# Adaptive LayerNorm, linear attention and a gated MLP on one core: a new planner model, LayerNorm transposes on TensorE, Ln/Exp reciprocals

## The chip, the cores and the metric

The kernel runs on one core of one Trainium2 chip. A core has TensorE (PE, matrix products into PSUM), VectorE (DVE), ScalarE (ACT), GpSimd (POOL) and SyncE (SP, which here only issues DMAs). The metric is the device time of one launch in microseconds. Each engine works through its own queue in the order in which the program put instructions there, and waits on semaphores for the other engines.

## The reference

One batch of S = 2048 rows, D = 512, H = 32 heads of 16, F = 1376. A condition vector c gives six vectors of scale, shift and gate.

```python
mod = silu(c) @ w_mod                  # sa, ca, ga, sb, cb, gb
h = layernorm(x) * (1 + ca) + sa
x = x + ga * A(h)
h = layernorm(x) * (1 + cb) + sb
x = x + gb * B(h)

# A: q, k, v = h @ wqkv, then per head
phi(p) = concat(softmax(p @ w_phi), softmax(-p @ w_phi))
kv = sum_s phi(k)^T v;  z = sum_s phi(k)
o = (phi(q) kv) / (phi(q) . z + 1e-6);  A = o @ wo
# B
B = (sigmoid(h @ w_gate) * (h @ w_up)) @ w_down
```

All of phi(k) of the 2048 rows goes into kv and z before the first row of the output can be formed. Nothing behind it can start sooner except the queries.

## The kernel before

Rows are worked on in 16 tiles of 128. The program is not written in order: `Graph.add` collects some thousand tasks, each with the engines that may run it and a duration for each, what it reads and writes, its buffers, a due time `due` and an earliest time `rel`. `Graph.order` (L87) plays the tasks through on a model of the engines: at each model time, the free engine takes the ready task that is due first, and due times are pulled forward from the tasks that depend on it (L93). The order that comes out is the order of each engine's queue on the chip. In this model a task that ends frees its successors after `LAT` = 0.25 us, a transfer takes 1.9 us and its bytes at 380 GB/s, and VectorE and GpSimd don't disturb each other.

**Start.** Weights and x come over SP's queue (L544 to L557), x in four loads of four tiles. c is turned into its SiLU (c1 to c3), with a Tanh on ScalarE. The rows of w_mod give the shift and scale columns `modc` (L591, `modc1` for the first LayerNorm). w_phi is folded into the weights of k and q: transposes `tp_w` (L609) or DMA transposes (L619), products `fold_ps` (L626), copies into `wqk_f` (L632, L634).

**Tile loop.** For groups of four tiles: statistics (`st1`, L647 and L648, VectorE), 1/sqrt as a power on GpSimd (`rs1`, L653 and L654), normalised `xn` (L665 ScalarE, L667 VectorE, L669 GpSimd), a transpose into `h1T` (groups 0 and 1 on TensorE, `tp_h` L681; groups 2 and 3 by DMA, L672) and the modulation (`hm1`, L687 VectorE, L689 GpSimd, L691 ScalarE). Where xn isn't made by VectorE, `nmr` (L657) prepares minus mean times 1/sqrt. Then for each tile: K (L706), exponentials e and its inverse (L719, ScalarE), their sums over a head (L722) and reciprocals (L730) on VectorE, the product `phi` on GpSimd (L725, the last two tiles in halves that VectorE may take), V (L710), its copy `vaug` (L734), and the sum into `kvacc` (L278). The queries (Q, L767, in four blocks of four tiles; exponentials `eT`, L772), `ga` and `gb` (L744), and the products `wo` (L751) and `wd` (L756) with the gates lie beside it.

**From kv to the feed-forward stage.** `kvbd` is the masked copy of the sums (L290, L295). For each unit (tile 0, tile 1, then pairs): `sm` (L338) gives norm and denominator parts, `smS` is their copy (L342), `m`, `den`, its reciprocal and `cc` (L348 to L351) the factors. `num` (L363), `u` (L369), for tiles 0 and 1 a transposing product `tpo` and its copy (L380, L383), for the others their sum `o` on GpSimd (L387) and a DMA transpose (L390); the output `a_ps` (L396), the residual x1 (L401), its statistics (L405), `rs2` (L412, L413), `xn` (L428, L430), its transpose (`tp_x` L443 or by DMA, L435) and modulation (L450, L452).

**Feed-forward.** Chunks of 1, 1, 2, 4, 4 and 4 tiles: for each of 11 column blocks of F `g_ps` and `u_ps` (L471), tanh (L475, sigmoid as a half tanh), the gated product `hm` (L480, into the space of w_mod, two chunk buffers), then `y` (L491), which needs `wd`, the last residual (L500) and the store (L502). A bound on the exponents (L513 to L532) selects a safer second version of the whole, which is not run with these inputs.

Of the kernel before, what the change touches and what calls it, by code (L numbers as in the profile page):

```python
# [9 lines left out]
FP32 = mybir.dt.float32  # L10
BF16 = mybir.dt.bfloat16
# [19 lines left out]
QREL = [42.0, 50.0, 56.0, 64.0]  # L31
AREL = [0.0, 0.0, 62.0, 70.0, 77.0, 90.0, 100.0, 115.0, 125.0]
# [15 lines left out]
class Task:  # L48
    def __init__(self, name, alts, fn, due, rel, bufs, nbytes):
        self.name, self.alts, self.fn, self.due, self.rel = name, alts, fn, due, rel  # L50
        self.bufs, self.nbytes = bufs, nbytes
        self.deps, self.succ = set(), []
        self.ready = rel
        self.ndep = 0


class Graph:


    LAT = 0.25  # L60
    PE_OUT = 0.2
# [6 lines left out]
    def add(self, name, alts, fn, r=(), w=(), bufs=(), due=1e6, rel=0.0, nbytes=0):  # L68
        t = Task(name, alts, fn, due, rel, list(bufs), nbytes)
# [17 lines left out]
    def order(self):  # L87
# [8 lines left out]
        free_at = {e: 0.0 for e in ("PE", "ACT", "DVE", "POOL", "SP")}  # L96
        slots = {c: list(range(n)) for c, n in self.caps.items()}
        ready = [t for t in self.tasks if t.ndep == 0]
        events = [0.0]
        done = []  # L100
        out = []
        fifo = 0.0
        now = 0.0
        left = len(self.tasks)
        while left:
# [14 lines left out]
            held = set()  # L120
            for t in list(ready):
# [18 lines left out]
                free_at[e] = now + t.alts[e]  # L140
                t.end = free_at[e]
                if t.nbytes:
                    fifo = max(now + 1.9, fifo) + t.nbytes / 380e3
                    t.end = fifo
# [24 lines left out]
def kernel(  # L169
# [39 lines left out]
    flag = cst.tile([1, 1], INT32, name="flag")  # L209
    wmod_sb = cst.tile([P, KT, 6 * D], BF16, name="wmod_sb")  # L210
# [33 lines left out]
    pool.memset(mhalf[:], -0.5)  # L244

# [56 lines left out]
    def downstream(G, eT, base, first):  # L302
# [9 lines left out]
        for k in range(NC):  # L312
            for ft in range(FT):
# [4 lines left out]
                tm += {0: 0.3, 1: 0.3, 2: 0.5, 3: 0.4, 4: 0.4, 5: 0.0}[k]  # L318
        ydue = tm

        for p, tiles in enumerate(UNITS):
# [3 lines left out]
            d0 = gdue[k, 0] - 2.0  # L325
            rel = AREL[p] if first else 0.0
            sm = bank("sm", [P, 2, 256])
            smS = small("smS", [P, 2, 128])
# [13 lines left out]
            G.add(f"smS{p}", {"ACT": 0.16 + 0.11 * nt}, lambda e, sm=sm, smS=smS, nt=nt: act.copy(smS[:, 0:nt], sm[:, 0:nt, 0:128]), r=[("sm", p)], w=[("smS", p)], bufs=[sm, smS], due=d0)  # L342
# [536 lines left out]
```

## Time and profile before

| | |
|---|---|
| Time, median of 3 runs | 233.52 us (233.03 to 233.52) |
| The profiled execution's own time | 232.49 us |
| Its span, first to last instruction | 230.8 us |
| Mean granted clock of TensorE in the span | 0.982 |
| Busy: PE, DVE, ACT, POOL | 206.3, 172.3, 103.1, 82.4 us |
| Moved by DMA | 19.27 MB |

The profile shows one execution. A row of the timeline has start, length, engine, line, operation and tiles; in brackets is the idle time of the engine before it and who ended it. A row of the groups has a line, an operation and its shapes, the count, the busy time and the mean length of one in nanoseconds, then the idle time before them. A row of the windows has a stretch, its length, the busy time of PE, its weight loads, DVE, ACT and POOL with the number of instructions, the granted clock, the DMA share and GB/s. Neighbouring instructions of one kind are merged into one row (x16); a matmul is counted to its modelled end, so two in a row overlap.

### The profile page before, as it was taken

The page shows a single profiled execution, that of the slowest core. Times are in us where ns is not written, and L with a number is a line of the kernel's source. Part 1 is how long each engine was busy: PE and PEld are TensorE (multiplying, and loading weights), DVE is VectorE, ACT ScalarE, POOL GpSimd, SP SyncE. Part 2 cuts the span into 40 slices and gives each one's busy share as a digit, 9 for nine tenths or more (in the row PEclk, how much of TensorE's full clock was granted, in tenths as well). Part 3 has the DMA queues.
Part 4 walks back from the last instruction along what each step waited for, and adds up shares of the span by engine and source line. Part 5 has one row for each costly group of instructions (what it writes and reads, how often), then busy time and mean ns, then how long its engine had stood idle before and what let it go on. Part 6 is the DMA issues. An engine that isn't in the chain of part 4 may idle for free.

```text
span 230.8 us, 4164 instructions
## 1 busy us (share of the span) xinstructions
PE 206.3 (89%) x1526; PEld 117.6 (51%) x1526; DVE 172.3 (75%) x355; ACT 103.1 (45%) x207; POOL 82.4 (36%) x91
## 2 busy tenths in 40 slices
PE   0588798899889769999999999999999999999990
PEld 0563555355445457876877544445454444444430
DVE  0689998759997998978999974958677988432430
ACT  2578685879785546443453233252321432322100
POOL 6405599679499725323200620110430300000000
PEclk9999999999999967999999999999999999999998
DMA  6974836059900002113222220132202061000011
GB/s 173 366 285 91 313 141 97 0 103 378 341 6 3 0 0 48 24 27 71 45 68 57 46 59 3 26 68 68 48 0 68 0 104 47 12 1 23 27 59 43
DMA packets 30333, 19.27 MB, mean 83 GB/s; under 512 B 22257, under 2 KB 27746, under 8 KB 30306
## 3 DMA queue, kind: packets, MB, share of 16 engines
q1 hardware_dynamic: 30272, 18.91, 29.1%
q8 instruction: 14, 0.23, 0.4%
q0 software_dynamic: 32, 0.02, 0.2%
q14 instruction: 13, 0.11, 0.2%
q10 hardware_dynamic: 2, 0.00, 0.0%
HBM read 11.58 MB, written 2.10 MB: 59 GB/s over the span
## 4 chain that ended last, share of the span: by engine, by line
PE 60%; ACT 0%; DVE 0%; issue 0%
PE u_ps L471 17%; PE g_ps L471 17%; PE y_ps L491 16%; PE a_ps L396 6%; PE num L363 2%; PE sm L338 1%; ACT eT L772 0%; PE q_ps L767 0%; DVE ot L500 0%; PE tp_x L443 0%; PE bnd L526 0%
## 5 line engine op out<-in xcount | busy, mean ns | idle before, releaser
L475 ACT ACTIVATE tg<-g_ps 128x512 bf16<-128x512 f32 (+5 forms) x66 | 29.5, 454 | 70.1 <-PE g_ps L471 59.1
L480 DVE SCALAR_TENSOR_TENSOR wmod_sb<-tg,u_ps 128x512 bf16<-128x512 bf16 (+5 forms) x66 | 32.3, 503 | 25.8 <-PE u_ps L471 21.7
L491 PE MATMUL y_ps<-wd_sb,wmod_sb 128*128 128x512 bf16 (+1 forms) x176 | 44.4, 379 | 0.0
L725 POOL TENSOR_TENSOR phi<-e,ks 128x1024 bf16<-128x1024 bf16 (+1 forms) x15 | 28.3, 1898 | 11.3 <-DVE ks L730 5.0
L471 PEld LDWEIGHTS <-wg_sb 128*128 128x128 bf16 (+1 forms) x264 | 23.5, 100 | 17.3 <-DVE wT_sb L450 0.5
L471 PEld LDWEIGHTS <-wu_sb 128*128 128x128 bf16 (+1 forms) x264 | 23.6, 100 | 16.4 <-issue 0.8
L387 POOL TENSOR_TENSOR o<-u 128x512 bf16<-128x512 f32 x14 | 17.9, 1287 | 35.6 <-DVE u L369 33.9
L471 PE MATMUL g_ps<-wT_sb,wg_sb 128*128 128x512 bf16 (+3 forms) x132 | 27.0, 326 | 0.0
L471 PE MATMUL u_ps<-wT_sb,wu_sb 128*128 128x512 bf16 (+3 forms) x132 | 26.8, 326 | 0.0
L491 PEld LDWEIGHTS <-wmod_sb 128*128 128x128 bf16 (+1 forms) x176 | 16.9, 98 | 17.5
L471 PE MATMUL u_ps<-wqk_sb,wu_sb 128*128 128x128 bf16 (+5 forms) x132 | 22.1, 290 | 0.5 <-ACT eT L772 0.5
L471 PE MATMUL g_ps<-wqk_sb,wg_sb 128*128 128x128 bf16 (+5 forms) x132 | 22.2, 290 | 0.0
L369 DVE TENSOR_TENSOR u<-num,cc 128x512 f32<-128x512 f32 (+1 forms) x32 | 20.6, 679 | 1.2 <-PE num L363 1.1
L722 DVE TENSOR_REDUCE ks<-e 128x64 f32<-128x1024 bf16 (+1 forms) x18 | 19.0, 1064 | 2.2 <-ACT e L719 2.2
L719 ACT ACTIVATE e<-k_ps 128x512 bf16<-128x512 f32 x32 | 17.2, 611 | 5.0 <-PE k_ps L706 3.4
L772 ACT ACTIVATE eT<-q_ps 128x512 bf16<-128x512 f32 x32 | 16.7, 621 | 3.7 <-PE q_ps L767 2.6
L706 PE MATMUL k_ps<-wqk_f,h1T 128*128 128x512 bf16 x64 | 16.2, 380 | 1.5 <-ACT h1T L691 0.8
L396 PE MATMUL a_ps<-wo_sb,oT 128*128 128x512 bf16 x64 | 16.1, 394 | 0.7 <-ACT eT L772 0.7
L412 POOL TENSOR_SCALAR ve<-mv 128x2 f32<-128x2 f32 (+1 forms) x9 | 2.0, 225 | 41.1 <-DVE mv L406 39.9
L710 PE MATMUL v_ps<-wv_sb,h1T 128*128 128x512 bf16 x64 | 16.1, 379 | 0.1
L767 PE MATMUL q_ps<-h1T,wqk_f 128*128 128x512 bf16 x64 | 15.5, 379 | 0.0
L500 DVE TENSOR_TENSOR ot<-y_ps,x 128x512 bf16<-128x512 f32 x16 | 11.0, 686 | 5.9 <-PE y_ps L491 5.8
(110 smaller groups left out, 280.8 us busy)
## 6 DMA issues: line engine op xcount, KB each, us to landing
x_sb<-in_A_x_dram SPq DMA_DIRECT2D x4, 512.0 KB, 9.9
wmod_sb<-in_w_mod_dram SPq DMA_DIRECT2D x1, 2048.0 KB, 8.0
out_dram<-ot SPq DMA_DIRECT2D x16, 128.0 KB, 1.8
wg_sb<-in_B_w_gate_dram SPq DMA_DIRECT2D x1, 1376.0 KB, 7.5
wu_sb<-in_B_w_up_dram SPq DMA_DIRECT2D x1, 1376.0 KB
wd_sb<-in_B_w_down_dram SPq DMA_DIRECT2D x1, 1280.0 KB, 13.5
wqk_sb<-in_A_wqkv_dram SPq DMA_DIRECT2D x2, 512.0 KB, 5.9
wmod_sb<-in_w_mod_dram SPq DMA_DIRECT2D x1, 1024.0 KB, 8.4
```

Of the source, the lines that this page charges most:

```text
L369: dve.tensor_tensor(u[:], ps[:].rearrange("p (h d) -> p h d", d=DH), cc[:, q, s, :].unsqueeze(2).to_broadcast([P, H, DH]), op=ALU.mult)
L387: G.add(f"o{t}", {"POOL": 1.3}, lambda e, ub=ub, o=o: pool.tensor_tensor(o[:], ub[0][:].rearrange("p h d -> p (h d)"), ub[1][:].rearrange( ...
L396: pe.matmul(ap_[:], lhsT=oT[:, j, :], rhs=wo_sb[:, j, :], start=(j == 0), stop=(j == KT - 1))
L471: pe.matmul(ps[:fsz, 0:n], lhsT=w[:, j, ft * P:ft * P + fsz], rhs=h[:, j, 0:n], start=(j == 0), stop=(j == KT - 1))
L475: G.add(f"tg{k}.{ft}", {"ACT": 0.15 + n * 0.00088}, lambda e, tg=tg, g_ps=g_ps, fsz=fsz, n=n: act.activation(tg[:fsz, 0:n], g_ps[:fsz, 0:n ...
L480: dve.scalar_tensor_tensor(hm_all[:fsz, hm[k].slot, ft, 0:n], tg[:fsz, 0:n], 1.0, u_ps[:fsz, 0:n], op0=ALU.add, op1=ALU.mult)
L491: pe.matmul(y[:], lhsT=hm_all[:fsz, hm[k].slot, ft, tl * P:(tl + 1) * P], rhs=wd_sb[:fsz, ft, :], start=(ft == 0), stop=(ft == FT - 1))
L706: pe.matmul(kp[:], lhsT=h1T[:, j, t * P:(t + 1) * P], rhs=wqk_f[:, j, D:2 * D], start=(j == 0), stop=(j == KT - 1))
L719: act.activation(ee[:, s].rearrange("p h j -> p (h j)"), kp[:], ACT.Exp, scale=1.0 - 2.0 * s)
L722: dve.tensor_reduce(ks[:, a:b], ee[:, a:b], axis=AX.X, op=ALU.add)
L725: engine(e).tensor_tensor(ph[:].rearrange("p (s h j) -> p s h j", s=2, j=DH)[:, a:b], ee[:, a:b], ks[:, a:b].unsqueeze(3).to_broadcast([P, ...
L772: act.activation(eT[cq][:, s * 4 + blk, :], qp[:], ACT.Exp, scale=1.0 - 2.0 * s)
```

## The change

All due and release times become constants of their own (`KD`, `LGD`, `GSL`, `UD`, `MISC`, `QREL`, `AREL`), and lists name the engines that each xn, hm1 and reciprocal may use. Beside these numbers:

- The planner: `LAT` 0.2, all engines start at 0.8, transfers at rates that rise with time, a DMA transpose holds SP for 1.2 us and lands after 2.5; a task whose engine is in its `port` list (GpSimd as a rule; VectorE too for xn, the SBUF modulations of LN2 and its xn) starts only when no other such task runs.
- Start: x tiles 0 to 3 in two loads, the first half of w_mod in two loads with its matmuls in two parts; Silu by Exp and a reciprocal instead of Tanh; 6 + 16 warm-up matmuls whose product isn't used; the zeros in the last block of w_down are set by VectorE at the start.
- LN1 in groups of 1, 1 and then 2 tiles, every one transposed on TensorE and modulated from PSUM; 1/sqrt as Ln and Exp on ScalarE for the first three groups, on ScalarE or GpSimd for the others.
- The reciprocals of phi(k): on VectorE, or as Ln and Exp on ScalarE; phi on GpSimd alone; wo on GpSimd alone; wd released from 78.45 on.
- The denominators: only half of `sm` is copied; m and cc read PSUM; the sum of two is a reduction.
- Table sets: one with Ln and Exp is loaded first, one with Tanh (`tsw`) behind the last reciprocal and the first rs2, which is now Ln and Exp on ScalarE.

```diff
-QREL = [42.0, 50.0, 56.0, 64.0]
-AREL = [0.0, 0.0, 62.0, 70.0, 77.0, 90.0, 100.0, 115.0, 125.0]
+T0, KP, GL = 11.57, 2.64, 7.92
+LG = [[0], [1], [2, 3], [4, 5], [6, 7], [8, 9], [10, 11], [12, 13], [14, 15]]
+QREL = [43.49, 61.34, 57.73, 11.53]
+AREL = [-41.36, 49.26, 40.7, 68.7, 71.54, 83.02, 104.54, 113.86, 145.92]
+RS1 = [{"ACT": 0.4}] * 3 + [{"POOL": 1.1, "ACT": 0.4}] * 6
...
+WDREL, WDDUE, WDSTEP = 78.45, 153.49, 1.05
...
+                if engs and all(e in t.port for e in engs) and port_free > now + 1e-9:
+                    port_wait = True
+                engs = [e for e in engs if e not in t.port or (port_free <= now + 1e-9 and not port_wait)]
...
+    act.preload_act_table_set("natural_log_exp_and_others")
...
-            G.add(f"smS{p}", {"ACT": 0.16 + 0.11 * nt}, lambda e, sm=sm, smS=smS, nt=nt: act.copy(smS[:, 0:nt], sm[:, 0:nt, 0:128]), r=[("sm", p)], w=[("smS", p)], bufs=[sm, smS], due=d0)
+            G.add(f"smS{p}", {"ACT": 0.17 + 0.06 * nt}, lambda e, sm=sm, smS=smS, nt=nt: act.copy(smS[:, 0:nt], sm[:, 0:nt, 64:128]), r=[("sm", p)], w=[("smS", p)], bufs=[sm, smS], due=d0)
...
-                dve.tensor_tensor(m[:, 0:nt], smS[:, 0:nt, 0:64], smS[:, 0:nt, 64:128], op=ALU.mult)
-                dve.tensor_tensor(den[:, 0:nt], m[:, 0:nt, 0:32], m[:, 0:nt, 32:64], op=ALU.add)
+                dve.tensor_tensor(m[:, 0:nt], sm[:, 0:nt, 0:64], smS[:, 0:nt], op=ALU.mult)
+                dve.tensor_reduce(den[:, 0:nt], m[:, 0:nt].rearrange("p q (s h) -> p q h s", h=32), axis=AX.X, op=ALU.add)
                 dve.reciprocal(den[:, 0:nt], den[:, 0:nt])
-                dve.tensor_tensor(cc[:, 0:nt], smS[:, 0:nt, 64:128].rearrange("p q (s h) -> p q s h", h=32),
+                dve.tensor_tensor(cc[:, 0:nt], sm[:, 0:nt, 64:128].rearrange("p q (s h) -> p q s h", h=32),
...
+                if e == "ACT":
+                    act.activation(ve2[:, sl], mv2[:, sl, 1], ACT.Ln, bias=eps[:, 0:1])
+                    act.activation(rs2[:, sl], ve2[:, sl], ACT.Exp, scale=-0.5)
...
+                G.add("tsw", {"ACT": 1.5}, lambda e: act.preload_act_table(ACT.Tanh),
+                      r=[("rs2", 0)] + [("kr", t, a) for t in range(NT) for a in range(2)], w=["tsw"], due=d0 + 3)
...
-    T0, KP = 13.0, 2.45
-    GB = T0 + NT * KP + 19.0
+    GB = T0 + NT * KP + GL
...
+    load_x("x0a", 0, 2, -20.0)
     load("wk", ["wk"], lambda e: sp.dma_start(wqk_sb[:, :, D:2 * D], wqkv_v[:, :, D:2 * D]), 512 * K1, -19.0)
+    load_wm(0, -18.5)
+    load_wm(1, -18.0)
+    load_x("x0b", 2, 4, -17.0)
...
+    def warm(nm, n, dur, **kw):
+        ps = bank("warm")
+
+        def f(e):
+            for _ in range(n):
+                pe.matmul(ps[:], lhsT=wd_sb[:, FT - 1, 0:P], rhs=wd_sb[:, FT - 1, :], start=True, stop=True)
+        G.add(nm, {"PE": dur}, f, bufs=[ps], **kw)
+    warm("warm0", 6, 2.4, r=["wdz"], w=["warm"], due=-40.0)
+    for i, rel in enumerate(WARM):
+        warm(f"warm1_{i}", 1, 0.22, r=["c1"], w=["warm"], due=MISC[3], rel=rel)
...
-            if g > 1:
-                G.add(f"xT1_{t}", {"SP": 0.1}, lambda e, t=t, xn=xn: sp.dma_start_transpose(h1T[:, :, t * P:(t + 1) * P], xn[:]),
-                      r=[("xn1", t)], w=[("h1raw", t)], bufs=[xn], due=gd, nbytes=250e3)
...
+            def f_r(e, ks=ks, a=a, b=b):
+                if e == "ACT":
+                    act.activation(ks[:, a:b], ks[:, a:b], ACT.Ln)
+                    act.activation(ks[:, a:b], ks[:, a:b], ACT.Exp, scale=-1.0)
+                else:
+                    dve.reciprocal(ks[:, a:b], ks[:, a:b])
...
-        G.add(f"wo{j}", {"POOL": 1.2, "DVE": 0.65}, lambda e, j=j: engine(e).tensor_tensor(wo_sb[:, j, :], wo_sb[:, j, :], ga_sb[:], op=ALU.mult),
-              r=["gac", "wo_raw"], w=[("wo", j)], bufs=[ga_sb], due=GB - 8.0, rel=48.0)
+        G.add(f"wo{j}", {"POOL": 1.28}, lambda e, j=j: engine(e).tensor_tensor(wo_sb[:, j, :], wo_sb[:, j, :], ga_sb[:], op=ALU.mult),
+              r=["gac", "wo_raw"], w=[("wo", j)], bufs=[ga_sb], due=GB + MISC[5], rel=50.0)
```

More of the change, by code (lines that the diff above doesn't have):

```diff
@@ L674 @@
+            G.add(f"xn1_{t}", alts, f_xn, r=[("rs1", g)] + ([("nmr1", g)] if set(alts) != {"DVE"} else []), w=[("xn1", t)],
+                  bufs=[xn], due=gd, port=("POOL", "DVE"))
         for j in range(KT):
[L675 to L682 removed]
```

240 lines of the change are left out of this document (143 added, 97 removed).

## The prediction

> **What bounds the kernel now.** I read the page first, then busy time by stage, then the chain that ended last, in order of time.
>
> ```profile
> PE   0588798899889769999999999999999999999990
> ```
> ```profile
> 14.30:69.85 55.55, 48.96 (x364) 26.46 (x363) 50.12 (x80) 43.45 (x83) 40.55 (x29) 1.00 0.54 162
> 69.85:90.20 20.35, 17.25 (x174) 11.20 (x172) 18.18 (x37) 10.50 (x23) 13.10 (x13) 0.83 0.05 8
> 90.20:224.50 134.30, 133.76 (x911) 73.86 (x909) 96.76 (x222) 42.33 (x88) 22.53 (x28) 1.00 0.18 41
> ```
> ```profile
> 216.90 7.58 PE y_ps L491 x35
> 224.51 0.69 DVE ot L500
> ```
>
> One slice is 5.8 us. TensorE is full from slice 16 on, and the chain of waits ends in 35 matmuls for y and one VectorE instruction. The windows (columns: length, busy PE, PEld, DVE, ACT, POOL, clock, DMA) give three stages: the loop over the 16 row tiles (14.3 to 69.85), the way from the last kv sum to the first gate matmul (69.85 to 90.2, clock 0.83), and the feed-forward stage, where TensorE is busy 133.76 of 134.30 us. The last stage can't shrink: the change takes no matmul out of it. Whatever is gained is gained by starting it earlier, and every microsecond there is one of the total, as long as the other engines still feed it and no work is pushed into it.
>
> **The start.**
>
> ```profile
> 0.80 0.40 SPq L544 DMA_DIRECT2D x_sb<-in_A_x_dram  x1
> 10.13 1.01 PE L591 MATMUL modc_ps<-sc_bf,wmod_sb 128*128 128x1 bf16 x32 [1.03 <-DMA wmod_sb<-in_w_mod_dram]
> 11.01 1.87 PE L626 MATMUL fold_ps<-bd,wT_sb 128*128 128x128 bf16 x16
> 12.67 1.81 PE L681 MATMUL tp_h<-ident,xn 128*128 128x128 bf16 x16
> 15.30 1.71 PE L706 MATMUL k_ps<-wqk_f,h1T 128*128 128x512 bf16 x7 [0.60 <-DVE h1T L687]
> 24.72 0.94 PE L626 MATMUL fold_ps<-bd,wT_sb 128*128 128x128 bf16 x12
> ```
> ```profile
> 7.20:14.30 7.10, 6.05 (x80) 5.79 (x81) 4.65 (x12) 4.75 (x11) 2.40 (x3) 1.00 1.04 391
> ```
>
> The first tile now waits in a row for w_mod (10.13), its matmuls, four folds, a four-tile transpose and four 512-wide modulations; steady K work starts at 15.30. Afterwards x comes in halves, so 1,792 KB instead of 2,048 lie ahead of the end of w_mod: 262 KB at 391 GB/s, 0.67 us less. Half of the modulation matmuls run before that (0.5 us), the folds no longer stand behind them (1.87), and the first transposes and modulations are for one tile, not four: 1.3 us less at 1.81 for sixteen. That sums to 4.3; as the folds were partly beside the DMA wait, I take **3.7**: first K at 11.6. Splitting x and w_mod puts two more issues of some 0.4 us on SP's queue; all loads up to w_mod's second half are issued by 3 us, long before they are wanted, so this is hidden. The last rows of w_down now wait for the warm-up matmuls too, which are over 40 us before that load is released. Bounds: 2.0 (the DMA order and the smaller group alone) to 4.3. The warm-up: sixteen matmuls took 1.87 us here and twelve 0.94 at 24.72, so the early ones ran at about two thirds of the later pace, although the clock column says 1.00. By these rows a warm start is worth 0.6 us for the folds, which is inside the 3.7; below, it could cost 0.4 if the last extra matmul stands ahead of a transpose. The Trainium skill ("TensorE: Matmul & The Clock Gate", Part 1) says that the array runs at half rate until it has been busy for a window of about 3.4 us. By that rule the warm-up of 22 matmuls would be enough and worth about 0.9 us on the folds; the pace above agrees in direction, the profile's clock column doesn't.
>
> **The tile loop.**
>
> ```profile
> L725 POOL TENSOR_TENSOR phi<-e,ks 128x1024 bf16<-128x1024 bf16 x14 | 27.3, 1958 | 11.3 <-DVE ks L730 5.0 <-ACT h1T L691 2.7 <-DVE nmr L657 1.8
> L722 DVE TENSOR_REDUCE ks<-e 128x64 f32<-128x1024 bf16 x14 | 16.6, 1183 | 2.2 <-ACT e L719 2.2
> L730 DVE RECIPROCAL ks<-ks 128x64 f32<-128x64 f32 x14 | 7.7, 550 | 0.4
> L751 DVE TENSOR_TENSOR wo_sb<-wo_sb,ga_sb 128x512 bf16<-128x512 bf16 x3 | 4.4, 1503 | 0.0
> L725 DVE TENSOR_TENSOR phi<-e,ks 128x512 bf16<-128x512 bf16 x3 | 4.0, 1349 | 0.0
> L687 DVE TENSOR_SCALAR h1T<-tp_h,modc 128x512 bf16<-128x512 bf16 x4 | 2.0, 533 | 0.0
> L657 DVE SCALAR_TENSOR_TENSOR nmr<-mv,rs 128x4 f32<-128x4 f32 x2 | 1.2, 610 | 0.0
> L342 ACT COPY smS<-sm 128x128 f32<-128x128 f32 x2 | 0.5, 266 | 0.0
> L450 DVE TENSOR_SCALAR wT_sb<-tp_x,modc 128x128 bf16<-128x128 bf16 x2 | 0.6, 334 | 0.0
> L667 DVE TENSOR_SCALAR xn<-x_sb,mv,rs 128x512 bf16<-128x512 bf16 x8 | 4.3, 603 | 1.9 <-POOL rs L654 1.9
> L570 ACT ACTIVATE c_ps<-c_ps 128x4 f32<-128x4 f32 x1 | 0.2, 158 | 0.1
> L570 ACT ACT_TABLE_LOAD x1 | 1.3, 1283 | 1.3 <-PEq L863 1.3
> ```
> ```profile
> 31.04 1.93 POOL L725 TENSOR_TENSOR phi<-e,ks 128x1024 bf16<-128x1024 bf16 x1
> 31.87 1.12 DVE L657 SCALAR_TENSOR_TENSOR nmr<-mv,rs 128x4 f32<-128x4 f32 x1
> 33.87 16.26 SPq L672 DMA_TRANSPOSE h1T<-xn  x8
> 40.95 0.73 DVE L687 TENSOR_SCALAR h1T<-h1T,modc 128x512 bf16<-128x512 bf16 x2 [1.02 <-DMA h1T<-xn]
> ```
>
> VectorE is the fullest engine of this stage: 50.12 of 55.55 us. It loses the wo products (4.4), the phi halves (4.0) and about half of the reciprocals, which now go to ScalarE (8 x 0.55 = 4.4). The DMA transposes of x go: eight took 16.26 us on SP's queue, the modulation of tiles 8 to 11 waited 1.02 us for them, and the loads of the gate weights behind them start sooner. In return TensorE has 32 more transposes, and all 36 modulations read PSUM: two thirds of them on VectorE, mostly 256 wide, some 0.38 each (between the 533 ns for 512 and the 334 for 128) are 9.1 against 3.6 now (4 x 0.53 and 4 x 0.37). nmr goes from two instructions to nine. One of the two took 1.12 us and ended with GpSimd's phi (31.04 + 1.93): while GpSimd runs, such an instruction waits. The new planner gives nmr no such price; six of the nine follow a GpSimd rs1 and meet the next phi, so I charge 6 x 1.0 = 6. Balance: 50.1 - 12.8 + 5.5 + 6 - 2 (a good third of the eight xn of 603 ns goes to other engines) = 46.8. GpSimd gets the phi halves, wo and some xn and loses the start of wd; at 40.55 of 55.55 us it has room for the 3 to 5 us that this makes. A reciprocal on ScalarE is two small instructions; no row has Ln. The nearest small one takes 266 ns, so 0.53; the bounds are 0.32, two of the 158 ns row, and 1.06, twice that for Ln and Exp each. ScalarE has 12 us idle here and loses the later queries, so this is free. At an occupation of 0.92 (now 0.90), 46.8 us of VectorE are a loop of about 51 us; from 12.5 us, when the first K is out, that ends kv at **63.5**, 6.3 earlier than 69.85, the 3.7 of the start included. Bounds: 60 (nmr never locked, waits gone) to 68 (start alone with some of it lost).
>
> The Trainium skill ("SBUF — State Buffer", section "SBUF: two separate sides") says that VectorE and GpSimd lock a shared port pair for a whole instruction, that the loser blocks, and that this holds for VectorE instructions with two SBUF inputs. The nmr row agrees. By this rule each of the nine nmr can be hit, which speaks against a planner that leaves it out; without that charge the loop would end about 6 us earlier.
>
> **From kv to the first gate.**
>
> ```profile
> L348 DVE TENSOR_TENSOR m<-smS 128x64 f32<-128x64 f32 x2 | 1.5, 762 | 0.8 <-ACT smS L342 0.8
> L349 DVE TENSOR_TENSOR den<-m 128x32 f32<-128x32 f32 x2 | 2.1, 1054 | 0.1
> L351 DVE TENSOR_TENSOR cc<-smS,den 128x64 f32<-128x64 f32 x2 | 1.5, 729 | 0.1
> L349 DVE TENSOR_TENSOR den<-m 128x64 f32<-128x64 f32 x7 | 1.6, 225 | 0.2
> L351 DVE TENSOR_TENSOR cc<-smS,den 128x128 f32<-128x128 f32 x7 | 2.0, 292 | 0.2
> L756 POOL TENSOR_TENSOR wd_sb<-wd_sb,wmod_sb 128x512 bf16<-128x512 bf16 x11 | 13.7, 1281 | 0.0
> ```
> ```profile
> 78.55 1.03 PE L396 MATMUL a_ps<-wo_sb,oT 128*128 128x512 bf16 x4
> 83.30 0.68 DVE L401 TENSOR_TENSOR x<-a_ps,x_sb 128x512 f32<-128x512 f32 x1
> 85.52 1.86 PE L396 MATMUL a_ps<-wo_sb,oT 128*128 128x512 bf16 x4 [0.75 <-ACT eT L772]
> 86.01 0.54 DVE L430 TENSOR_SCALAR xn<-x,mv,rs 128x512 bf16<-128x512 f32 x1
> 88.45 0.63 PE L443 MATMUL tp_x<-ident,xn 128*128 128x128 bf16 x4
> ```
> The one-tile m, den and cc take 2.5 us a unit, more than the two-tile forms with twice the elements, because they ran beside the eleven wd products; they now read PSUM or are a reduction, and wd comes later. At the two-tile prices a unit costs 0.8: 1.7 less, two units 3.4. The first x1 stood 3.7 us behind its matmul (79.58 to 83.30), queued on VectorE behind others' den and u; its xn, done at 86.55, waited 1.9 more for TensorE, which was in order behind the second output at half clock (1.86 us for four). LN2's first rs2 moves from GpSimd to ScalarE, 0.5 less. Together 9.5, but part of the queueing comes back, since the same work of units 1 and 2 has to be done then; I take **7**: 13.4 us instead of 20.35. Bounds: 0 and 9.5. The Tanh table set is now loaded (the one load now, at the start, took 1.28 us) between rs2 and the first modulations; xn and transpose cover 1.1 of it; uncovered it would cost 1.3. It waits for that rs2 and for all reciprocals of the loop; queued behind it on ScalarE are half of the first modulations and the first tanh.
>
> **The sum.** First gate at 63.5 + 13.4 = 76.9, 13.3 earlier. But TensorE must then do in 65 us (11.6 to 76.9) what it has been busy with for 48.96 + 17.25 = 66.2 us, some 3.5 of that lost to the slow clock (0.17 of 20.35), and 32 more transposes (at most 3.4). No idle would be left, and waits in order leave at least 2: so some queries fall behind the first gate, 2 us. The gain is 13.3 - 2 = 11.3. wd costs nothing in this, if queries and gates cover it. Of the profiled execution (232.49: span 230.8 and 1.7 around it) that leaves 221.2, and in proportion to the median of the runs (233.52) **222**.
>
> **Rivals.**
> - *The forecast*, 218 to 226: chance 0.62.
> - *TensorE never waits.* For: wherever it waited, the work that could fill was there (queries). Against: 6.6 us idle in the loop now. Its work from 11.6 to the first gate is 66.2 - 3.5 + 2, less perhaps 3 (an estimate) because busy counts each matmul to its end: the gate comes at 73.3 with nothing left over, 5.6 better than 76.9 with 2 left: 216, range 213 to 218. Chance 0.13.
> - *The order doesn't fit the chip.* Queues are fixed by the planner; x1's 3.7 us shows what a misjudged order costs. If the way to the first gate keeps its 20 us and only the 6.3 come through (the queries then have room): 227, range 226 to 232. Chance 0.14.
> - *wd starves TensorE: slower.* wd's 11 products (13.7 us) go from beside the loop to behind 78 us, among the o sums, and each y of the first tile needs all eleven; two chunk buffers hold gated tiles, so chunk 2 waits for y of chunk 0. If GpSimd ends wd at 100 or later, TensorE, with 9.5 us of gates and ups for chunks 0 and 1 after 77 (176 matmuls of 128 columns, a quarter of 7.58/35 each) and 5.2 of outputs for four more tiles (16 of 7.58/35, 32 of a quarter), stands from about 92. It is slower than before from 11.3 us of such waits, wd done at 103; at 106 the time is 236. Against: 22.53 of 134 us are GpSimd's load there now, and queries fill. Chance 0.09.
> - *Nothing that counts*: gains and waits cancel within 0.2%, about what a measurement of this kernel tells from no change. Chance 0.02.
>
> **How the numbers follow.** The range takes the forecast and the near ends of both neighbours: 214 to 231; about 0.07 lies below and 0.12 above. Faster 0.87, same 0.03, slower 0.10.
>
> **What would show it.** Right: K steady by 12 us; no DMA transposes before the first gate except four of the query weights; kv's last matmul at 60 to 66; den instructions under 0.4 us; first gate by 74 to 80 with the clock at 1.00 in between; TensorE busy over 98% behind it. Wrong: nmr near 0.1 us each (the loop is then shorter), a den still over 0.7, TensorE waits on wd or hm between 80 and 105, more than two table loads, or a loop bound by ScalarE.

## The result and the profile after

The changed kernel takes 226.97 us (median of 4 runs, 226.6 to 228.33) against 233.28 for the kernel before beside it: a ratio of 0.9748, 95% interval 0.9697 to 0.98. The prediction said 222 and 214 to 231: a gain of 11.3 us was forecast, 6.3 were measured. The profiled execution took 226.69 us, its span is 224.9 (before: 230.8).

The page's slices of TensorE and of its granted clock, after (one slice is 5.6 us):

```profile
PE   7987979889999998999999999999999999999980
...
PEclk9999979999999999999999999999999999999997
```

TensorE is full from the tenth slice on, but for one at 8, instead of from the sixteenth, and the dip of the clock lies in the loop now (the sixth slice, 28 to 34 us) instead of on the way to the first gate.

The same three stages as in the prediction, and the tail, by windows (columns as there: length, busy PE, PEld, DVE, ACT, POOL, clock, DMA):

```profile
12.97:66.56 53.59, 48.42 (x379) 28.08 (x385) 45.60 (x88) 43.11 (x95) 41.18 (x35) 0.97 0.46 157
66.56:84.09 17.53, 17.41 (x179) 10.52 (x179) 16.06 (x42) 15.04 (x33) 9.97 (x11) 1.00 0.08 16
84.09:218.60 134.51, 132.97 (x906) 74.31 (x917) 96.80 (x217) 42.45 (x90) 31.43 (x35) 1.00 0.19 40
```

The loop starts 1.3 us earlier (12.97 for 14.30) and ends 3.3 earlier (66.56 for 69.85). The way to the first gate takes 17.53 us for 20.35, so that the gate comes 6.1 earlier. The last stage has kept its length, 134.51 for 134.30. What counts is in the second column: between kv and gate TensorE is busy for all but 0.12 us; before, 3.1 us were idle there and the clock was 0.83.

Split at 48 us instead of at the last kv sum, the kernel before and then the changed one:

```profile
14.30:48.00 33.70, 29.06 (x229) 15.85 (x228) 29.90 (x53) 25.39 (x48) 23.15 (x18) 1.00 0.49 133
48.00:90.20 42.20, 37.15 (x309) 21.82 (x308) 38.40 (x64) 28.56 (x59) 30.50 (x24) 0.92 0.34 112
```
```profile
12.97:48.00 35.03, 29.96 (x243) 17.38 (x247) 33.11 (x65) 28.60 (x64) 25.43 (x25) 0.95 0.70 239
48.00:84.09 36.09, 35.86 (x315) 21.22 (x317) 28.55 (x65) 29.55 (x63) 25.72 (x21) 1.00 0.04 9
```

From 48 us to the first gate the kernel before lost 5.0 us of TensorE to idle time and 3.4 to the clock (0.08 of 42.2); after, 0.2 are lost. That is 8.2 us gained, and the start adds 1.3. Given back ahead of the gate are 1.8 us of slow clock before 48 us (0.05 of 35) and 0.4 of idle time there. That leaves 7.3; the gate came 6.1 earlier, and the other 1.2 us are what is left for the 32 transposes that TensorE now has on top. A row of eight of them spans 0.62 us in this trace, so they may take up to 2.5: the account is good to about a microsecond. The last stage is 0.2 longer: the span is 5.9 shorter.

The clock terms say how much less work TensorE did in that stretch, not what the time would be without them. The changed kernel's five executions beside the first experiments (`c_after` below) had a mean granted clock of 0.995 and 0.996 (226.84 and 227.24 us), 0.985 and 0.986 (226.82 and 226.32 us) and 0.978 (228.49 us). From 0.996 to 0.985 is 2.5 us of clock (0.011 of 225) and nothing in time. For the kernel before, on the same chip, 0.995 to 0.996 went with 231.94 to 232.28 us and 0.974 to 0.976 with 233.01 to 233.14: some 4.7 us of clock, 1 us of time. That would fit slow stretches that fall where TensorE has to wait for other engines anyway; no run tests it.

The way from kv to the first gate, after (a VectorE and a TensorE timeline; start, length, then the operation):

```profile
66.30 0.48 DVE L339 SCALAR_TENSOR_TENSOR kvbd<-kvacc,bmask 128x24 bf16<-128x24 f32 x3 [4.87 <-PE kvacc L322]
...
75.44 0.68 DVE L445 TENSOR_TENSOR x<-a_ps,x_sb 128x512 f32<-128x512 f32 x1
...
76.99 1.87 DVE L413 TENSOR_TENSOR u<-num,cc 128x512 f32<-128x512 f32 x3
...
80.31 0.52 DVE L481 TENSOR_SCALAR xn<-x,mv,rs 128x512 bf16<-128x512 f32 x1
```
```profile
77.60 4.48 PE L845 MATMUL q_ps<-h1T,wqk_f 128*128 128x512 bf16 x20
81.92 0.39 PE L494 MATMUL tp_x<-ident,xn 128*128 128x128 bf16 x4
...
84.09 0.39 PE L522 MATMUL g_ps<-wqk_sb,wg_sb 128*128 128x128 bf16 x4
```

VectorE idles 4.87 us for the last kv sums. The first x1 is ready at 76.1, but its xn comes four microseconds later, behind the u, x1 and statistics of the next units. TensorE doesn't notice: it makes five late query blocks (77.60 to 82.08) meanwhile.

The groups of instructions that answer to the priced ones (columns: busy us, mean ns, idle before and its releaser):

```profile
L734 DVE SCALAR_TENSOR_TENSOR nmr<-mv,rs 128x2 f32<-128x2 f32 x7 | 4.4, 627 | 0.0
L746 POOL TENSOR_SCALAR xn<-x_sb,rs,nmr 128x512 bf16<-128x512 bf16 x8 | 6.2, 772 | 8.1 <-DVE nmr L734 7.9
L392 DVE TENSOR_TENSOR m<-sm,smS 128x64 f32<-128x64 f32 x2 | 0.4, 220 | 0.7 <-ACT smS L386 0.7
L393 DVE TENSOR_REDUCE den<-m 128x32 f32<-128x64 f32 x2 | 0.4, 220 | 0.1
L395 DVE TENSOR_TENSOR cc<-sm,den 128x64 f32<-128x64 f32 x2 | 0.4, 224 | 0.1
```

m, den and cc fell from 762, 1054 and 729 ns to 220, 220 and 224. The nmr is the other way round: an instruction on two columns takes 627 ns on average, from 0.1 us up to 1.61 us.

### The profile page after: what moved, and what is told of

Same layout as the page of the kernel before. It is cut to its first block, busy times and chain, and to the rows that moved or that the text cites. A ratio compares the mean times of both kernels' runs of the same rounds, so it can differ in the third digit from the quotient of the medians.

```text
span 224.9 us, 4268 instructions
## 1 busy us (share of the span) xinstructions
PE 210.1 (93%) x1558; PEld 118.9 (53%) x1580; DVE 165.5 (74%) x366; ACT 107.6 (48%) x233; POOL 87.0 (39%) x99
## 4 chain that ended last, share of the span: by engine, by line
PE 74%; DVE 19%; issue 3%; ACT 2%; DVEq 0%; ACTq 0%
PE y_ps L542 17%; PE u_ps L522 16%; PE g_ps L522 16%; PE a_ps L440 5%; PE v_ps L781 4%; PE k_ps L777 4%; PE warm L647 3%; DVE st L719 3%; DVE ks L793 2%; PE kvacc L322 2%; PE q_ps L845 2%; PE num L407 2%; DVE u L413 2%; DVE h1T L761 2%; DVE st L449 1%
## 5 line engine op out<-in xcount | busy, mean ns | idle before, releaser
L542 PE MATMUL y_ps<-wd_sb,wmod_sb 128*128 128x512 bf16 (+1 forms) x170 | 44.9, 379 | 0.5 <-ACT tg L526 0.2
L796 POOL TENSOR_TENSOR phi<-e,ks 128x1024 bf16<-128x1024 bf16 (+1 forms) x18 | 31.0, 1735 | 7.5 <-ACT ks L804 2.0
L522 PE MATMUL u_ps<-wqk_sb,wu_sb 128*128 128x128 bf16 (+3 forms) x175 | 31.0, 298 | 0.7 <-DVE wmod_sb L531 0.6
L522 PE MATMUL g_ps<-wqk_sb,wg_sb 128*128 128x128 bf16 (+3 forms) x173 | 30.8, 297 | 0.2
L781 PE MATMUL v_ps<-wv_sb,h1T 128*128 128x512 bf16 x58 | 17.0, 405 | 1.9 <-DVE h1T L761 1.5
L522 PE MATMUL u_ps<-wT_sb,wu_sb 128*128 128x256 bf16 (+3 forms) x87 | 17.8, 325 | 0.1
L522 PE MATMUL g_ps<-wT_sb,wg_sb 128*128 128x256 bf16 (+3 forms) x88 | 17.9, 326 | 0.0
L440 PE MATMUL a_ps<-wo_sb,oT 128*128 128x512 bf16 x61 | 15.1, 379 | 0.2
L845 PE MATMUL q_ps<-h1T,wqk_f 128*128 128x512 bf16 x63 | 14.7, 379 | 0.1
L479 ACT ACTIVATE xn<-x,nmr,rs 128x512 bf16<-128x512 f32 x14 | 10.7, 805 | 4.9 <-DVE nmr L465 4.9
```

The source lines that it names most:

```text
L440: pe.matmul(ap_[:], lhsT=oT[:, j, :], rhs=wo_sb[:, j, :], start=(j == 0), stop=(j == KT - 1))
L522: pe.matmul(ps[:fsz, 0:n], lhsT=w[:, j, ft * P:ft * P + fsz], rhs=h[:, j, 0:n], start=(j == 0), stop=(j == KT - 1))
L542: pe.matmul(y[:], lhsT=hm_all[:fsz, hm[k].slot, ft, tl * P:(tl + 1) * P], rhs=wd_sb[:fsz, ft, :], start=(ft == 0), stop=(ft == FT - 1))
L781: pe.matmul(vp[:], lhsT=h1T[:, j, t * P:(t + 1) * P], rhs=wv_sb[:, j, :], start=(j == 0), stop=(j == KT - 1))
L796: engine(e).tensor_tensor(ph[:].rearrange("p (s h j) -> p s h j", s=2, j=DH)[:, a:b], ee[:, a:b], ks[:, a:b].unsqueeze(3).to_broadcast([P, ...
L845: pe.matmul(qp[:], lhsT=wqk_f[:, j, blk * P:(blk + 1) * P], rhs=h1T[:, j, cq * 512:(cq + 1) * 512], start=(j == 0), stop=(j == KT - 1))
```

## The experiments

Each was timed against the kernel before on the same chip, in five rounds. "The control" is the changed kernel itself. Theories: **A**, from 48 us on TensorE is full, and what it loses before that is the whole loss; **B**, the loop's end and the way to the first gate set the time, as the prediction had it.

### The control, an earlier gate, and the planner's lock

`c_after` is the changed kernel. `x_gate` takes the port from the LN2 xn of the first unit, so that the planner puts it earlier; `x_nolock` takes the port out of the planner altogether.

```diff
-                      bufs=[x1[t], xn], due=d0 + 1 + q, port=("DVE",))
+                      bufs=[x1[t], xn], due=d0 + 1 + q, port=() if first and p == 0 else ("DVE",))
```
```diff
     def add(self, name, alts, fn, r=(), w=(), bufs=(), due=1e6, rel=0.0, nbytes=0, port=("POOL",)):
+        port = ()
```

> The changed kernel again, so that the runs beside it are compared on one chip. Both theories: 226 to 228 us. Theory A (TensorE's idle time): from about 48 us TensorE is never idle, as queries fill each wait, so only what it loses before that and between 84 and 100 us counts; the largest single cause is nmr on VectorE, planned at 0.16 us and met by GpSimd's phi three times (1.09, 1.16 and 1.61 us). Theory B (the way to the first gate): the time follows the last phi on GpSimd and the chain from there to the first gate matmul at 84.1.

> The planner no longer holds the first xn of the second LayerNorm back while GpSimd works, so that it and its transpose stand some two places earlier in their queues and the first gate matmul comes at about 82 instead of 84.1; the queries that stood before it come after it. Theory A: TensorE is full before and after, so the time stays at 226 to 228. Theory B: 2 us less, 224 to 226.

> The planner's lock between VectorE and GpSimd is taken out and nothing else, so that every queue is ordered without it; instructions and numbers of the change are the same. If the lock in the planner is what the change gains by, the chip again falls behind its plan and it is 229 to 234 us. If the other edits (transposes on TensorE, denominators from PSUM, table sets, wd later) carry the gain, it is 225 to 228.

Control: 226.84 us, ratio 0.9756 [0.973, 0.9781]. Its profiled execution took 228.49 us, and its loop ends at 68.4 instead of 66.56 as above: the same kernel, with more of its TensorE time lost before 48 us. Windows are best compared with both. x_gate: 227.66, 0.9782 [0.9754, 0.981]. x_nolock: 227.55, 0.9798 [0.9771, 0.9825]. A row of the gate's matmuls in the control and then in x_gate (behind the three lengths stand the first and the last start; the first gate is in both rows):

```profile
L522 PE MATMUL g_ps<-wqk_sb,wg_sb x176: 216/298/380, 85.9 to 209.8; 128*128 128x128 bf16 x80, 128*128 128x512 bf16 x80, 128*96 128x128 bf16 x8, 128*96 128x512 bf16 x8
```
```profile
L522 PE MATMUL g_ps<-wqk_sb,wg_sb x132: 219/273/380, 84.2 to 181.4; 128*128 128x128 bf16 x40, 128*128 128x256 bf16 x40, 128*128 128x512 bf16 x40, 128*96 128x128 bf16 x4
```

With the last kv matmul at the same place (its start at 68.2 and 68.0 us), the gate came 1.7 us earlier, and nothing was gained, as A had it: B falls for a gate that comes while TensorE is full. The planner orders what stands behind the gate anew as well, so this is one whole plan against another. So is x_nolock: the lock in the planner, named first in the change, is worth some 0.7 us there; the intervals overlap, and the other edits carry the gain.

### nmr off VectorE, twice

`x_nonmr` drops the nmr of LN1 from VectorE: GpSimd makes its xn as subtract and multiply, ScalarE makes nmr itself ahead of its xn. `x_nmr2` makes nmr on ScalarE at the same place of the order and leaves GpSimd's xn alone.

```diff
-                    pool.tensor_scalar(xn[:], x_sb[:, t, :], rs1[:, t:t + 1], nmr[:, 0, t:t + 1], op0=ALU.mult, op1=ALU.add)
+                    pool.tensor_scalar(xn[:], x_sb[:, t, :], mv1[:, t, 0:1], rs1[:, t:t + 1], op0=ALU.subtract, op1=ALU.mult)
```
```diff
-            G.add(f"nmr1_{g}", {"DVE": 0.16}, lambda e, sl=sl: dve.scalar_tensor_tensor(nmr[:, 0, sl], mv1[:, sl, 0], -1.0, rs1[:, sl], op0=ALU.mult, op1=ALU.mult),
+            def f_nmr(e, ts=ts, sl=sl):
+                for t in ts:
+                    act.activation(ve1[:, t:t + 1], mv1[:, t, 0:1], ACT.Identity, scale=rs1[:, t:t + 1])
+                act.mul(nmr[:, 0, sl], ve1[:, sl], -1.0)
+            G.add(f"nmr1_{g}", {"DVE": 0.16}, f_nmr,
```

> The same order of every queue, but nmr isn't made on VectorE any more: GpSimd's xn subtracts the mean itself, and where ScalarE makes xn it makes nmr too, with two small instructions. Theory A: VectorE gets back 3.4 us of waiting between 24 and 43 us, TensorE's idle time before 48 us falls from 5 to 2 or 3, the clock doesn't drop near 31 us, and the time is 223 to 225. Theory B: GpSimd ends the loop as late as now, within 1 us, and the time stays at 226 to 228.

> The nine small nmr instructions of LN1 leave VectorE; ScalarE makes them (mean times rs, then times -1) at the same place of the order, and GpSimd keeps its xn as multiply and add. Everything else as in the changed kernel, which takes 0.975 of the time before. Theory A (what TensorE loses before 48 us is the whole loss, and VectorE, the fullest engine there, makes it): 4.4 us of locked nmr go, TensorE is busy 1.5 to 3 us more between 12 and 48 us, and the time falls by 1.5 to 3 us: ratio 0.962 to 0.969. Rival C (GpSimd's chain of phi bounds the loop, so VectorE's lock time is idle time by another name): within 0.7 us of the changed kernel, ratio 0.972 to 0.978.

x_nonmr: 229.78 us, 0.9884 [0.9861, 0.9906], slower than the control, against what both theories said. The reason is in one group:

```profile
L748 POOL TENSOR_SCALAR xn<-x_sb,mv,rs 128x512 bf16<-128x512 bf16 x8 | 16.6, 2081 | 5.0 <-ACT rs L727 5.0
```

Subtract and multiply took 2081 ns where multiply and add takes 772: 10.4 us more on GpSimd. So the run can't tell what nmr is worth.

x_nmr2: 223.83 us, 0.9629 [0.96, 0.9659], 3 us faster than the control. Windows of the changed kernel (the execution shown in the first section), then of x_nmr2:

```profile
12.00:48.00 36.00, 30.66 (x246) 17.72 (x251) 34.08 (x68) 29.57 (x66) 25.43 (x25) 0.95 0.71 244
```
```profile
12.00:48.00 36.00, 31.39 (x269) 18.39 (x272) 32.91 (x66) 33.33 (x89) 28.24 (x26) 1.00 0.71 247
```

TensorE is busy 0.7 us more before 48 us, and its clock doesn't fall (0.05 of 36 are 1.8 us): 2.5 us more of work by then. The missing slow stretch isn't the cause of the gain: x_nmr2's five executions at 0.994 to 0.998 took 223.18 to 224.35 us, and the control's two at 0.995 and 0.996 took 226.84 and 227.24 (the kernel before took 232.4 on both chips). VectorE is busy 1.2 us less and gets further; the last kv matmul ends at 63.8 us instead of 66.56. ScalarE pays 3.8 us in this window and has the room. The time is what A said; of the 1.5 to 3 us that TensorE was to be busier, 0.7 came, and 1.8 against the control's 29.57. C as it was put, no gain, falls. But GpSimd too had been waiting for nmr (7.9 us in the group above) and now does 2.8 us more in the same time, so this run doesn't show which of the two engines had to be freed.

### The reciprocals back on VectorE

```diff
             def f_r(e, ks=ks, a=a, b=b):
+                e = "DVE"
```

> All reciprocals of the loop on VectorE, none as Ln and Exp on ScalarE, in the same order. VectorE gets about 5 x 0.55 us and some halves, near 3.5 us in all, mostly before 55 us. Theory A (VectorE makes TensorE's idle time before 48 us): 1.5 to 3 us longer than the changed kernel, ratio 0.981 to 0.988. Rival C (GpSimd's phi chain bounds the loop, VectorE has the gaps): within 0.7 us, ratio 0.972 to 0.979.

228.91 us, 0.985 [0.9822, 0.9877]: 2.1 us longer than the control, as A had it. Its window:

```profile
12.00:48.00 36.00, 30.18 (x233) 17.55 (x235) 35.55 (x67) 26.23 (x55) 23.73 (x23) 0.91 0.71 245
```

VectorE has no gap left (35.55 of 36 us), TensorE idles 5.8 us and runs at 0.91. This profiled execution took 228.46 us, the control's 228.49, its slowest of five: the window shows where the time goes, and the 2.1 us are read from the medians. Here only VectorE got more to do, which speaks for it as the engine that holds the loop before 48 us. ScalarE, with 26 to 30 of 36 us in these windows, has room for the Ln and Exp.

### The small sums, and where wd stands

`x_denold` brings back the forms of before (all of m, den and cc from SBUF); `x_wdearly` puts the eleven wd right behind wo in GpSimd's queue; `b_wdlate` is the kernel **before** with wd moved back alone.

```diff
-                dve.tensor_tensor(m[:, 0:nt], sm[:, 0:nt, 0:64], smS[:, 0:nt], op=ALU.mult)
-                dve.tensor_reduce(den[:, 0:nt], m[:, 0:nt].rearrange("p q (s h) -> p q h s", h=32), axis=AX.X, op=ALU.add)
+                dve.tensor_tensor(m[:, 0:nt], smS[:, 0:nt, 0:64], smS[:, 0:nt, 64:128], op=ALU.mult)
+                dve.tensor_tensor(den[:, 0:nt], m[:, 0:nt, 0:32], m[:, 0:nt, 32:64], op=ALU.add)
...
```
```diff
     order = G.order()
+    wds = [t for t in order if t.name.startswith("wd") and t.name[2:].isdigit()]
+    order = [t for t in order if t not in wds]
+    at = 1 + max(i for i, t in enumerate(order) if t.name in ("wo3", "gbc"))
+    order[at:at] = wds
```
```diff
     order = G.order()
...
+    for a, b, behind in ((0, 5, "o3"), (5, 11, "rs2_1")):
+        at = 1 + order.index(by_name[behind])
+        order[at:at] = [by_name[f"wd{i}"] for i in range(a, b)]
```

> The small sums go back to their forms before: all 128 columns copied by ScalarE, and m, den and cc read and write SBUF alone, so they can be locked out by GpSimd; order unchanged. Units 0 and 1 run while GpSimd makes the wo products, so each den step should again be near 0.7 to 1 us. Theory A (behind 48 us TensorE is never idle; queries cover a late first gate): first gate 1.5 to 3 us later, time within 0.7 us of the changed kernel, ratio 0.972 to 0.979. Theory B (the way from the last kv sum to the first gate sets the time, as the prediction had it): 1.7 to 3 us longer, ratio 0.982 to 0.989.

> All eleven wd products go on GpSimd right behind wo, as before the change, instead of from 78 us on; the rest of the order is unchanged. GpSimd stood idle for 7.2 us between wo and the first o in the changed kernel (72.3 to 79.6 in the control run), so about six of them fit there and the first o comes some 5 to 6 us later, 16 x1 tiles hang on such o. Theory A (TensorE is full from 48 us on and queries cover what comes late, as with the later first gate): within 0.7 us of the changed kernel, ratio 0.972 to 0.979. Theory D (by 85 us no queries are left to cover, so whatever delays the first chunks there is paid in full): TensorE idles 2 to 5 us between 80 and 105 us and the time grows by 2 to 5 us: ratio 0.984 to 0.998.

> The kernel before, with one part of the change alone: five of the eleven wd products stand behind the first two o on GpSimd and six behind the next rs2, instead of right behind the last phi; all else as before. Theory D (where wd stands is what the change is worth, whatever the forms beside it): m, den and cc of units 0 and 1 meet an idle GpSimd (225 to 290 ns each instead of 730 to 1050), the first gate comes 3 to 4 us earlier, y of the first tile waits a little for wd: 1.5 to 3.5 us shorter, ratio 0.985 to 0.994. Rival E (in the old order GpSimd's wd did not hold up o, which waits for u there; wd behind o now ends near 100 us, just where y wants it, and VectorE meets the lock in the later units instead): within 1 us of the kernel before or slower, ratio 0.996 to 1.015.

x_denold: 230.27 us, 0.9908 [0.9874, 0.9942], 3.4 us longer: A's forecast of no difference failed, and the loss is a little above B's 1.7 to 3 us, at another place than B had it. VectorE and TensorE of x_denold:

```profile
69.45 0.66 DVE L392 TENSOR_TENSOR m<-smS 128x64 f32<-128x64 f32 x1 [0.77 <-ACT smS L386]
70.14 1.05 DVE L393 TENSOR_TENSOR den<-m 128x32 f32<-128x32 f32 x1
...
84.64 1.25 DVE L392 TENSOR_TENSOR m<-smS 128x128 f32<-128x128 f32 x1
85.92 1.06 DVE L393 TENSOR_TENSOR den<-m 128x64 f32<-128x64 f32 x1
...
88.09 0.58 DVE L501 TENSOR_SCALAR wqk_sb<-tp_x,modc 128x128 bf16<-128x128 bf16 x2
```
```profile
88.47 0.47 PE L522 MATMUL g_ps<-wqk_sb,wg_sb 128*128 128x128 bf16 x3 [2.38 <-DVE wqk_sb L501]
```

The first unit's m and den were locked out by wo (0.66 and 1.05 us for 0.22 each), which the queries still covered but for 0.7 us. The den of later units met wd at 84.6 and pushed the modulation behind them to 88.1. TensorE, whose five query blocks were done by then, stood 2.4 us with one gate matmul issued, and its clock was 0.89 from 84 to 100 us (at half from 89 to 93): another 1.8.

x_wdearly: 232.03 us, 0.9987 [0.9962, 1.0012], 5.2 us longer: nearly the whole gain, and just above theory D's 2 to 5 us (that by 85 us no queries are left to cover a delay). GpSimd, then TensorE:

```profile
69.82 12.57 POOL L834 TENSOR_TENSOR wd_sb<-wd_sb,wmod_sb 128x512 bf16<-128x512 bf16 x11
82.34 2.49 POOL L431 TENSOR_TENSOR o<-u 128x512 bf16<-128x512 f32 x2
```
```profile
76.96 4.48 PE L845 MATMUL q_ps<-h1T,wqk_f 128*128 128x512 bf16 x20
81.27 0.39 PE L494 MATMUL tp_x<-ident,xn 128*128 128x128 bf16 x4
86.09 1.89 PE L440 MATMUL a_ps<-wo_sb,oT 128*128 128x512 bf16 x4 [4.43 <-DMA oT<-o]
```

The o of tiles 2 and 3 come 2.8 us later than the control's (79.57). TensorE has their output ahead of the first gate in its order, and stands 4.43 us with the five query blocks done; the clock is 0.79 from 84 to 100 us. A fails here: its cover has an end, as D had it.

b_wdlate: 234.83 us, 1.0078 [1.0049, 1.0108], 0.8% slower than before: D's gain didn't come, rival E's range did. Its groups of single-tile sums, and a window of the kernel before and then of b_wdlate:

```profile
L348 DVE TENSOR_TENSOR m<-smS 128x64 f32<-128x64 f32 x2 | 0.4, 221 | 0.8 <-ACT smS L342 0.8
L349 DVE TENSOR_TENSOR den<-m 128x32 f32<-128x32 f32 x2 | 0.4, 194 | 0.1
```
```profile
84.00:100.00 16.00, 14.75 (x179) 11.56 (x177) 14.96 (x41) 9.38 (x27) 6.93 (x8) 0.83 0.15 29
```
```profile
84.00:100.00 16.00, 10.30 (x107) 8.69 (x107) 11.55 (x28) 4.69 (x16) 15.92 (x16) 0.79 0.09 18
```

The old den takes 194 ns for 1054 with an idle GpSimd, and the first gate comes at 84.3 instead of 90.2. But from 84 to 100 us TensorE does 4.4 us less. The placing is coarser than the planner's (five wd stand ahead of the second rs2 here, and VectorE waits 2.62 us for it), so it is no fair price of the move; it does show that a gate 5.9 us earlier can go with a longer time.

### The warm-up and the last phi

`x_nowarm` issues none of the 22 warm-up matmuls; `x_phidve` gives the second phi halves of tiles 14 and 15 to VectorE, which waits for the last kv sums there.

```diff
-            for _ in range(n):
-                pe.matmul(ps[:], lhsT=wd_sb[:, FT - 1, 0:P], rhs=wd_sb[:, FT - 1, :], start=True, stop=True)
+            pass
```
```diff
+                if t >= SPLIT and a == 1:
+                    e = "DVE"
```

> None of the 22 warm-up matmuls is issued; order unchanged. Theory A: the first folds, transposes and K run at half pace for some 3 to 4 us more and the first K is 0.5 to 1.5 us later, which all comes through: ratio 0.978 to 0.983. Rival (the prediction's bound: the warm start is worth 0.6 on the folds only, and the loop waits for VectorE anyway): within 0.5 us, ratio 0.973 to 0.978.

> The second halves of the phi products of tiles 14 and 15 go from GpSimd to VectorE, which waits 4.9 us for the last kv sum there; order unchanged. The last kv matmul comes about 1.5 to 2 us earlier. Theory A (from 48 us on TensorE is never idle, so an earlier kv only moves queries behind it): within 0.7 us of the changed kernel, ratio 0.972 to 0.979. Theory B (the loop's end and the way to the first gate set the time, as the prediction had it): 1.5 to 2 us shorter, ratio 0.966 to 0.969.

x_nowarm: 226.88 us, 0.9766 [0.9718, 0.9814]: no difference clear of the noise, as the rival had it, and hardly a later first K (13.19 for the control's 13.01). The pace did change. The first sixteen transposes of the changed kernel and then of x_nowarm:

```profile
7.67 1.06 PE L678 MATMUL tp_w<-ident,wqk_sb 128*128 128x128 bf16 x16
```
```profile
6.18 1.89 PE L677 MATMUL tp_w<-ident,wqk_sb 128*128 128x128 bf16 x16 [3.47 <-DMA wqk_sb<-in_A_wqkv_dram]
```

So the warm-up makes these matmuls 0.8 us shorter, but the first K isn't much earlier for it, and the time shows no gain. With an interval of 1.1 us to either side, a gain of the 0.6 us that was priced can't be excluded.

x_phidve: 227.73 us, 0.979 [0.9752, 0.9828]: no clear difference either, and the last kv matmul started at 68.0 like the control's 68.2, although phi was ready earlier. GpSimd's last phi of x_phidve, then TensorE:

```profile
64.77 1.51 POOL L798 TENSOR_TENSOR phi<-e,ks 128x512 bf16<-128x512 bf16 x1 [0.86 <-PE kvacc L322]
```
```profile
66.75 1.03 PE L824 MATMUL gb_ps<-wmod_sb,scb 128*128 128x512 bf16 x4
67.62 0.64 PE L322 MATMUL kvacc<-vaug,phi 128*128 128x136 bf16 x8
```

GpSimd is done at 66.28 (the control: 67.08) and VectorE's halves at 65.36, but TensorE comes to the last kv matmuls without a wait, behind the products for ga and gb in its queue; it is busy 20.00 of the 20 us from 48 to 68. So it is TensorE's queue, not phi, that sets the end of the loop there. The edit couldn't give the earlier kv that should have told A from B; what it shows is A's full TensorE.

### A new order on top of x_nmr2

`x_order` is x_nmr2 with its tasks swapped one by one, and 30 of them given to another engine, against a replay with durations from x_nmr2's trace; the result stands in the kernel as a list.

```diff
     order = G.order()
+    by_name = {t.name: t for t in order}
+    order = [by_name[n] for n in ORDER]
...
+        t.eng = {"P": "PE", "A": "ACT", "D": "DVE", "G": "POOL", "S": "SP"}[ENGS[p]]
...
```

> As the kernel with nmr on ScalarE (ratio 0.963), with a new order and other choices of engine for 30 tasks, found by swapping tasks of its order against durations and pitches read from that kernel's trace, with the lock between VectorE and GpSimd counted. If theory A holds, what is left to gain is TensorE's idle time between 12 and 48 us (4.6 us in that kernel) and about 1 us behind the first gate: the replay has TensorE 3 us busier there, the last kv sum 3 us earlier and the first gate at 78.5 instead of 81.4: 2.5 to 4 us shorter, 220 to 221.5 us, ratio 0.946 to 0.953. Rival: the order fits the durations that it was made from and not the chip, and waits in order take it back: 223 to 226 us, ratio 0.959 to 0.972.

221.58 us (221.26 to 221.94), 0.9529 [0.9498, 0.9561]: faster than both kernels. The control has 0.9756 of the time before, some 5.3 us more. A's 220 to 221.5 us is met at its upper end. Its windows:

```profile
12.00:48.00 36.00, 33.15 (x280) 19.37 (x281) 34.98 (x68) 33.53 (x87) 29.72 (x28) 1.00 0.71 244
48.00:79.80 31.80, 31.76 (x284) 18.39 (x282) 25.37 (x58) 26.62 (x58) 27.40 (x23) 1.00 0.04 9
79.80:213.40 133.60, 133.55 (x923) 74.30 (x921) 95.77 (x216) 43.15 (x91) 26.21 (x31) 1.00 0.18 41
```

TensorE is busy 33.15 us in the window that had 31.39 in x_nmr2 and 30.66 in the changed kernel, the clock is 1.00, and it loses 0.1 us from 48 us to the last y. VectorE is at 34.98 of 36 us in the first window: what is left lies there.

## Why the prediction was right, and where not

**The last stage is fixed, the gain comes ahead of it.** Right: 134.51 us for 134.30, and even x_order has 133.60.

**The numbers.** The measured time lies outside the forecast's own 218 to 226 and inside 214 to 231, which takes in the near end of the rival at 227. Of the signs, den under 0.4 us, two table loads, the clock at 1.00 on the way to the gate and TensorE at 98.9% behind it came; the three times (K by 12, kv by 66, gate by 80) didn't.

**The start, 3.7 us.** Too much. Counted as the prediction did, from the steady K at 15.30 to the first K, it was 1.5 (13.83, with the first V ahead of it at 12.97), in the control 2.3. The trace suggests why: modc stood at 11.5 us, and half of the first modulations waited on VectorE behind the statistics of tile 2 (11.09 to 11.91). This order wasn't tried by itself. The warm-up, priced at up to 0.6, has no worth that x_nowarm could show (its interval is 1.1 us to either side). By the Trainium skill's rule of half rate until the array has been busy for a while ("TensorE: Matmul & The Clock Gate", Part 1) the prediction estimated 0.9; x_nowarm's slower first matmuls (1.89 us for 1.06) agree with the rule; its time neither shows nor excludes the gain.

**nmr, 6 us of VectorE.** Right in kind, near in size: 4.4 us busy, against 1 if none were locked (three of the nine were held up, by 1 to 1.5 us each, not six), and 3 us of time by x_nmr2 (223.83). The Trainium skill's rule that VectorE and GpSimd lock a shared port pair ("SBUF — State Buffer", "SBUF: two separate sides") agrees here and in b_wdlate's den (194 ns beside an idle GpSimd, 1054 before). The nmr is the part of the change's own model that was left out: that model charges 0.16 us and no lock.

**The loop at VectorE's occupation of 0.92.** This step failed. Its load was right (46.8 forecast, 45.60 measured), its occupation was 0.85, and kv ended at 66.56, not 63.5. The two parts of the loop differ; the second, beside the row from 12.97 to 48 us above:

```profile
48.00:66.56 18.56, 18.45 (x137) 10.70 (x138) 12.49 (x24) 14.51 (x31) 15.75 (x11) 1.00 0.01 2
```

Up to 48 us VectorE is occupied to 0.95 (33.11 of 35.03), more than forecast. Then TensorE is the full engine (18.45 of 18.56), and VectorE only to 0.67; its 4.87 us at the end are a wait for TensorE's queue, in which the last kv matmuls follow without a gap, 0.65 us behind GpSimd's last phi (65.27). The forecast let one engine bound the whole loop. Without the nmr lock kv ends at 63.8.

**The way to the first gate, 7 us shorter.** The prices were right (220 ns each for m, den and cc); it took 17.53 us for 13.4 because the saved time went to the next units' work on VectorE. And the size didn't matter as the prediction had it: 1.7 us earlier gave nothing (x_gate), 2.4 us of TensorE's waiting went with 3.4 of time (x_denold).

**TensorE's budget.** This was the step that decided, with the right mechanism: no idle time would be left, so the end follows from TensorE's work and what it loses. From 48 us to the gate it lost 0.23 us, but ahead of that the idle time was mis-sized: it lost not 2 us but 5.2 idle in the loop (53.59 less 48.42) and 1.6 to the clock (0.03 of 53.59). Against the forecast's 78.9 us (76.9 and 2 of spilled queries) the gate came 5.2 later: 1.4 by the start, 3.2 by the idle time, 1.6 by the clock, and 1.0 came back. (The sum was not quite kept: 11.6 + 66.2 - 3.5 + 3.4 and 2 of waits are 79.7, so only 2.6 of the 3.4 for transposes are in 78.9.) That is the difference between 222 and 227, as an account of work; after the executions above, the clock's 1.6 us need not all have been time to gain.

**wd costs nothing.** Right, but it was a narrow thing: its old place in the new order costs 5.2 us. It didn't starve TensorE behind the gate (15.05 of 15.91 us busy there), so the slower rival didn't come.

**"The order doesn't fit the chip, 227."** The number came, but not the reason, so the agreement is chance: the way to the gate didn't keep its 20 us. The gate is 6.1 us earlier, 3.3 of it from the loop and 2.8 from the way to the gate, and the queries fill both.

**The parts.** Taken out one at a time, the planner's lock, the reciprocals on ScalarE, the small sums and the late wd cost 0.7, 2.1, 3.4 and 5.2 us, together twice the 5.6 us that the control gains: so such prices can't be added. The transposes on TensorE, the smaller groups, the split loads and the table sets weren't taken out alone; what each is worth isn't shown.

## What to carry to other kernels

Ask first from which moment the bounding engine is never idle. Time saved behind that moment is only paid out as far as that engine was waiting; what counts is the work that it has done by then. Work that can fill (here five query blocks) covers a late step up to its own length and no further: a gate 1.7 us earlier was worth nothing, and a stand of 2.4 us behind the last query block went with 3.4 us of time (x_denold). The two-column nmr held the fullest engine for 1.09 to 1.61 us three times, at a planner's price of 0.16: look at the mean length of small instructions in the groups before trusting a price. And compare executions of one kernel at different clocks before a slow stretch is counted as time lost.

## What was not expected of the hardware

- GpSimd's tensor_scalar on 128x512 bf16 took 2081 ns as subtract and multiply and 772 as multiply and add.
- Behind a stand of TensorE its clock was low: 2.4 us in x_denold and 4.43 in x_wdearly went with a clock of 0.89 and 0.79 over 16 us, 1.8 and 3.4 us of clock. In x_wdearly the clock fell in the middle of the stand, so some 2.5 of the 3.4 lie behind it.
- The gap alone doesn't decide: the changed kernel and the control both stood 1.27 us ahead of the same folds (at 28.9 and 28.0 us); the clock of the first was at half from 31 to 34 us, that of the control stayed at 1.00 until 36.
- Ln and Exp on 128x64 took 256 and 257 ns on ScalarE, each about half of VectorE's reciprocal (550), with two table loads in all (1283 ns each).
